# A spectral filter with two feed-forward networks: filter units over 48 slots, spectrum sums on VectorE, output gate turned on TensorE

## The chip, the cores and the metric

One Trainium2 chip, one core of it. The engines are TensorE (PE in the profile, with its weight loads as PEld), VectorE (DVE), ScalarE (ACT), GpSimd (POOL) and SyncE (SP, which here only issues DMAs). The metric is the time of one execution on the device in microseconds, the median of the runs shown.

## The reference

```python
def _attn_ref(x, filt_r, filt_i):            # x: 8 x 3072 x 256
    X = np.fft.rfft(x, axis=1)
    y = np.fft.irfft(X * (filt_r + 1j * filt_i)[None], n=x.shape[1], axis=1)
    return y.astype(np.float32)

def _moe_ref(x, w_in, w_out):                # 24576 x 256 -> 2048 -> 256
    h = x @ w_in
    g = np.where(h > 0.0, h, np.exp(np.minimum(h, 0.0)) - 1.0)
    return (g @ w_out).astype(np.float32)

def _moe2_ref(x, w_gate, w_output_gate, w1, w2):   # 8 experts, 256 -> 1024 -> 256
    logits = x @ w_gate
    e_idx = np.argmax(logits, axis=1)
    ...
    gate_w = probs[np.arange(N), e_idx]
    eom = 1.0 / (1.0 + np.exp(-(x @ w_output_gate)))
    for e in range(E):
        mask = e_idx == e
        h = np.maximum(x[mask] @ w1[e], 0.0)
        out[mask] = gate_w[mask, None] * eom[mask, e, None] * (h @ w2[e])
```

The three follow each other: a filter along the sequence for 8 batches, a feed-forward network, and a network of 8 experts in which each token goes to one.

## The kernel before

The program has three stages. The **start** filters batch 0, from which the second stage takes its first input. Its order comes from the compiler's scheduler. The **main loop** has 768 slots; its order is written out by hand. The **expert stage** works through the tokens in about 100 blocks of 256; the change leaves it alone but for where the table of the output gate comes from.

**A slot of the main loop.** 48 chunks of 512 tokens have 16 slots each. Slot t runs, in this order: the side work planned for it, `mm1(t)` (6 matmuls of 512 columns into one of two PSUM buffers `h`, then on ScalarE a Relu and an Exp into `e`, then on VectorE the step `e`, which reads `h` and so frees it), `split_g(t-1)` (a rounded copy of `e` on ScalarE and the rest, `g`, on VectorE), and `mm2(t-3)` (12 matmuls of 264 columns into four accumulators `z`). Side work marked for TensorE stands at the slot's end. Each engine works in order, so side work of slot t on VectorE stands ahead of step `e` of slot t; `mm1(t+2)` needs the `h` that step `e` of slot t frees. Once in 16 slots come the emptying of `z` into `rt`, the gate (`gate1` to `gate3`) and the scatter of rows to DRAM by GpSimd, and VectorE's two halves of the next chunk's input (`ys`, L637); every 11 slots a piece of the experts' weights is prepared (`prep_*`, with L767 on GpSimd).

**A filter unit** is one half (128 columns) of one batch, b = 1 to 7, two for each 96 slots. Its parts:

- `fft.load`: 16 DMAs of x into tile `X` (1.5 MB).
- `f1`, `f2`: 12 and 9 VectorE steps of 128 to 1536 elements, from `X` through `AA` into `AT` (L173 to L195).
- six pairs of frequencies, each through `PAIR`: `ld` (tables `cf`, filter `fl`), `hi`, `lo`, `neg`, `fwd` (12 matmuls), `mul` (VectorE, with the filter), `add` and `ylo` (GpSimd, L285, L286, L299), `yhi`, `inv` (12 matmuls with table `ci`), `evac`.
- `b1`: 20 steps of VectorE that join the pairs' results in `Z`, and two DMAs to `yd`, from which later chunks are loaded.

`plan_unit` puts `f1` in slots t0 to t0+7, `f2` in t0+8 and t0+9, pair i in t0+9+3i and on, `b1` in t0+33 to t0+42, three pieces of `f1` in two slots and two of `b1` in one; units of a batch start 43 slots apart, and 10 of 96 slots have none. `cf`, `fl`, `ci`, `X`, `AT` and `Z` have one buffer each. SyncE issues nearly all DMAs from one queue, in order.

**The output gate.** The expert stage needs `w_output_gate` with its rows and columns exchanged (`wogT`). A DMA from GpSimd's queue does that at the start, element by element (L921).

Of the kernel before, what the change touches and what calls it, by code (L numbers as in the profile page):

```python
# [9 lines left out]
F32 = mybir.dt.float32  # L10
F32R = mybir.dt.float32r
# [5 lines left out]
ALU = mybir.AluOpType  # L17
# [14 lines left out]
R8 = float(np.sqrt(0.5))  # L32
S3 = float(np.sqrt(0.75))
# [60 lines left out]
class Fft:  # L94
# [35 lines left out]
    def unit(self, b, h, own=None):  # L130
# [4 lines left out]
        nc, one, st, big = self.nc, self.one, self.st, self.big  # L135
        v, tt, stt = nc.vector, nc.vector.tensor_tensor, nc.vector.scalar_tensor_tensor
# [64 lines left out]
        P = {}  # L201
# [79 lines left out]
        def add(i):  # L281
            p = P[i]
            a, c = p["a"], p["b"]
            Y = p["Y"] = a
            nc.gpsimd.tensor_tensor(out=Y[:, :, 0], in0=a[:, :, 0], in1=c[:, :, 1], op=ALU.subtract)  # L285
            nc.gpsimd.tensor_tensor(out=Y[:, :, 1], in0=a[:, :, 1], in1=c[:, :, 0], op=ALU.add)  # L286

        def yhi(i):
            p = P[i]
            if not own:  # L290
                off, n = self.off[i]
                k = p["k"] = st.tile([W, 1792], F32R, tag="ci", name="ci")
                nc.sync.dma_start(out=k[:, 0:n].bitcast(F32), in_=self.inv_d[:, off:off + n])
# [101 lines left out]
        def eight(q, e, w):  # L395
# [142 lines left out]
def fft_moe_kernel(ctx, tc, x, filt_r, filt_i, w_in, w_out, wg, wog, w1, w2, out):  # L538
    nc = tc.nc
    v, g = nc.vector, nc.gpsimd  # L540
# [11 lines left out]
    wogT = dram.tile([NE * W, D], F32, name="wogT")  # L552
# [4 lines left out]
    ident = ct[:, 88:216]  # L557
# [10 lines left out]
    def bank():  # L568
        return pf.tile([W, 512], F32, tag="pf", name="pf")
# [36 lines left out]
    P1 = {}  # L606
# [13 lines left out]
    Y = {}  # L620
# [148 lines left out]
    def prep_st(n):  # L769
# [22 lines left out]
    def plan_unit(b, h, t0, nxt, early=False):  # L792
        u = fft.unit(b, h)
        late = {}
        for n, q in enumerate(u["f1"]):
            late.setdefault(t0 + n * 8 // len(u["f1"]), []).append(q)
        for n, q in enumerate(u["f2"]):
            late.setdefault(t0 + 8 + n // 5, []).append(q)
        if nxt:
            late.setdefault(t0 + 10, []).append(lambda: fft.load(*nxt))  # L800
        for t, fns in late.items():
            for fn in fns:
                at(t, fn)
        for t in range(9, 33):
            for i in range(6):
                for nm, d in sorted(PAIR, key=lambda q: -q[1]):
                    if 9 + 3 * i + d == t:
                        at(t0 + t, lambda nm=nm, i=i: u[nm](i), nm in ("fwd", "inv"))
# [59 lines left out]
    cf, ci = {}, {}  # L868
# [414 lines left out]
```

## Time and profile before

| | |
|---|---|
| time, median of 3 runs | 3935.37 us (3932.18 to 3935.83) |
| the profiled execution | 3930.68 us, its span 3928.8 us |
| TensorE busy | 3730.6 us, 95% of the span |
| VectorE busy | 2426.4 us, 62% |
| ScalarE busy | 2071.2 us, 53% |
| GpSimd busy | 908.9 us, 23% |
| granted clock, mean of the span | 0.987 |
| start, to the first matmul of `mm1` | 137.8 us |
| main loop | 137.8 to 2702.1 us |
| expert stage | 2702.1 to 3928.8 us |

Busy shares are averages over the three stages; a matmul counts as busy to its modelled end, so 95% doesn't say that nothing can be gained.

### The profile page before, as it was taken

The numbers are of one execution on the slowest core, as the hardware profiler recorded it, in microseconds if no ns is written. First come the engines' busy times: TensorE is split into PE (matmuls) and PEld (weight loads), VectorE is DVE, ScalarE is ACT, GpSimd is POOL, SyncE is SP. The second block draws the span as 40 slices with busy tenths as digits, with TensorE's granted clock in tenths as the row PEclk, the third lists the DMA queues.
The fourth block names the chain that finished last, engine by engine and source line by source line (L and its number), as shares of the span: only waits on it lengthen the run. The fifth ranks groups of instructions, "written<-read, shape, count | busy, mean of one in ns | idle before, by whom it ended". The sixth has DMA issues, their size and how long they took to land. (4 is left out here: it accounts for less than half of the span.)

```text
span 3928.8 us, 70310 instructions
## 1 busy us (share of the span) xinstructions
PE 3730.6 (95%) x26359; PEld 3494.2 (89%) x26359; DVE 2426.4 (62%) x4761; ACT 2071.2 (53%) x3896; POOL 908.9 (23%) x1019
## 2 busy tenths in 40 slices
PE   2799999999999999999999999997999999999998
PEld 2688998988889889899898988997999999999998
DVE  5878778777686876877868676554433433433433
ACT  2566666666666666666666666664333333333332
POOL 2532232222312223222222221111111111111111
PEclk9899999999999999999999999998999999999999
DMA  6543343333423424334243342200121221221221
GB/s 147 180 137 112 127 148 113 117 117 111 152 80 132 149 90 149 102 120 131 89 147 109 126 129 71 93 28 24 46 89 49 89 88 48 90 88 49 89 89 36
DMA packets 234945, 400.55 MB, mean 102 GB/s; under 512 B 21354, under 2 KB 153834, under 8 KB 228458
## 3 DMA queue, kind: packets, MB, share of 16 engines
q1 hardware_dynamic: 215706, 344.40, 28.4%
q0 software_dynamic: 18896, 51.62, 3.6%
q8 instruction: 210, 3.44, 0.4%
q14 instruction: 133, 1.09, 0.1%
HBM read 679.09 MB, written 114.78 MB: 202 GB/s over the span
## 5 line engine op out<-in xcount | busy, mean ns | idle before, releaser
L672 PEld LDWEIGHTS z<-wex,g 128*128 128x128 f32 x9216 | 1231.6, 189 | 85.5 <-DVE rt L690 16.8
L672 PE MATMUL z<-wex,g 128*128 128x264 f32 x9216 | 1256.7, 285 | 14.0 <-DVE rt L690 13.6
L649 PE MATMUL h<-ys,win 128*128 128x512 f32 x4608 | 1215.4, 399 | 49.0 <-DVE e L655 44.0
L649 PEld LDWEIGHTS h<-ys,win 128*128 128x128 f32 x4608 | 818.0, 189 | 201.7 <-DVE e L655 57.6
L655 DVE SCALAR_TENSOR_TENSOR e<-e,h 128x512 f32<-128x512 f32 x768 | 525.7, 684 | 643.0 <-ACT e L654 639.2
L653 ACT ACTIVATE e<-h 128x512 f32<-128x512 f32 x768 | 459.2, 598 | 687.3 <-PE h L649 644.9
L1201 PE MATMUL h<-zt,w1s 128*128 128x256 f32 x4800 | 593.4, 283 | 0.8 <-ACT zt L1169 0.7
L1218 PE MATMUL o<-w2s,hs 128*128 128x256 f32 x4800 | 585.1, 281 | 0.0
L1201 PEld LDWEIGHTS h<-zt,w1s 128*128 128x128 f32 x4800 | 583.6, 192 | 1.5 <-ACT zt L1169 1.1
L1218 PEld LDWEIGHTS o<-w2s,hs 128*128 128x128 f32 x4800 | 567.3, 188 | 0.0
L662 DVE TENSOR_TENSOR g<-e,g 128x512 fp32r<-128x512 f32 x768 | 548.9, 715 | 0.1
L654 ACT ACTIVATE e<-e 128x512 f32<-128x512 f32 x768 | 485.7, 632 | 24.4
L661 ACT CAST g<-e 128x512 fp32r<-128x512 f32 x768 | 465.7, 606 | 44.8 <-DVE e L655 44.2
L1206 DVE SCALAR_TENSOR_TENSOR hs<-h,hs 128x512 fp32r<-128x512 f32 x400 | 276.9, 692 | 313.8 <-ACT hs L1205 312.8
L1226 POOL DMA_INDIRECT out_dram<-o,rows x200 | 197.5, 988 | 994.7 <-ACT o L1225 591.1
L1205 ACT ACTIVATE hs<-h 128x512 fp32r<-128x512 f32 x400 | 239.3, 598 | 338.7 <-PE h L1201 334.8
L743 POOL DMA_INDIRECT rows_d<-rt,sl x192 | 202.8, 1056 | 555.2 <-DMA rows_d<-rt,sl 228.2
L1225 ACT ACTIVATE o<-o,ogv 128x256 f32<-128x256 f32 x200 | 84.0, 471 | 461.5 <-PE o L1218 461.5
L1181 DVE TENSOR_SCALAR ogv<-ogv 128x2 f32<-128x2 f32 x100 | 17.0, 170 | 384.9 <-ACT ogv L1180 384.9
L720 POOL TENSOR_TENSOR A<-A,ohb 128x8 bf16<-128x8 bf16 x192 | 73.9, 385 | 685.6 <-DVE rt L711 624.4
L299 POOL TENSOR_TENSOR YH<-fa,YH 128x512 fp32r<-128x512 f32 x88 | 115.3, 1310 | 209.1 <-ACT YH L295 208.3
L285 POOL TENSOR_TENSOR fa<-fa,fb 128x256 f32<-128x256 f32 x88 | 72.9, 828 | 274.1 <-DVE fa L279 148.1
(262 smaller groups left out, 3013.4 us busy)
## 6 DMA issues: line engine op xcount, KB each, us to landing
w1s<-wpk SPq DMA_DIRECT2D x200, 1024.0 KB
w2s<-wpk SPq DMA_DIRECT2D x200, 1024.0 KB
ci<-dft_inv SPq DMA_DIRECT2D x73, 768.0 KB
cf<-dft_fwd SPq DMA_DIRECT2D x87, 512.0 KB
wpk<-ps SPq DMA_DIRECT2D x64, 512.0 KB
rows<-rows_d SPq DMA_DIRECT2D x100, 258.0 KB
y<-yd SPq DMA_DIRECT2D x46, 512.0 KB
fl<-fs SPq DMA_DIRECT2D x84, 256.0 KB
```

Source lines behind the costliest of these rows:

```text
L649: nc.tensor.matmul(out=ps, lhsT=win_s(m // 4)[:, a, k, m % 4 * W:m % 4 * W + W], rhs=s[:, q, k], start=(n == 0), stop=(n == 5))
L653: nc.scalar.activation(out=e, in_=ps, func=AF.Relu, scale=-1.0)
L654: nc.scalar.activation(out=e, in_=e, func=AF.Exp, scale=-1.0)
L655: v.scalar_tensor_tensor(out=e, in0=e, scalar=-1.0, in1=ps, op0=ALU.add, op1=ALU.max)
L661: nc.scalar.copy(out=s[:, 0], in_=e)
L662: v.tensor_tensor(out=s[:, 1], in0=e, in1=s[:, 0].bitcast(F32), op=ALU.subtract)
L672: nc.tensor.matmul(out=Z[c][i], lhsT=s[:, q, i * W:i * W + W], rhs=wex_s(m // 4)[:, a, m % 4], start=(m == 0 and q == 0 and a == 0), stop= ...
L743: g.indirect_dma_start(out=rows_d, out_offset=bass.IndirectOffsetOnAxis(ap=f["sl"][:, i:i + 1], axis=0), in_=f["rt"][:, i, NE:NE + ROW], i ...
L1201: nc.tensor.matmul(out=ps[:, q * TB:q * TB + TB], lhsT=w1s[mp // 2][:, a, k, m * W:m * W + W], rhs=s[:, z, k], start=(n == 0), stop=(n == 5))
L1205: nc.scalar.activation(out=hs[:, 0, 2 * mp:2 * mp + 2], in_=p2, func=AF.Relu)
L1206: v.scalar_tensor_tensor(out=hs[:, 1, 2 * mp:2 * mp + 2], in0=p2, scalar=0.0, in1=hs[:, 0, 2 * mp:2 * mp + 2].bitcast(F32), op0=ALU.max, o ...
L1218: nc.tensor.matmul(out=pss[q], lhsT=hs[:, z, k, q * W:q * W + W], rhs=w2s[k // 4][:, a, k % 4], start=(k == 0 and n == 0), stop=(k == 7 an ...
```

## The change

It has three parts. **The plan of the units.** A unit has 48 slots and the pairs stand 4 slots apart (`GAP`). `f1` and `f2` of the next unit are done while this one's pairs run, `b1` after them is cut so that one third of it (`thirds(0, 1)`) is done among the pairs, and `level` spreads the steps by their sizes: it fills slot after slot up to a cap, counting what stands there already (`load_of`, and 1.4 us of credit where a `fwd` or `inv` makes the slot longer), and raises the cap until all fit. The loads are issued elsewhere: `X` at t0, to be used from t0+8 on; `cf` three slots ahead of its `fwd` (before two), `ci` three ahead of its `inv` (before two). **The sums and low parts of the spectrum** (`add`, `ylo`) are on VectorE, in the start too. **The output gate** is loaded as it lies, turned by two small matmuls with the identity in slot 15, copied by ScalarE and stored as rows in slot 17; the DMA at the start is gone.

```diff
         def add(i):
-            nc.gpsimd.tensor_tensor(out=Y[:, :, 0], in0=a[:, :, 0], in1=c[:, :, 1], op=ALU.subtract)
-            nc.gpsimd.tensor_tensor(out=Y[:, :, 1], in0=a[:, :, 1], in1=c[:, :, 0], op=ALU.add)
+            tt(out=Y[:, :, 0], in0=a[:, :, 0], in1=c[:, :, 1], op=ALU.subtract)
+            tt(out=Y[:, :, 1], in0=a[:, :, 1], in1=c[:, :, 0], op=ALU.add)
...
         def ylo(i):
-            nc.gpsimd.tensor_tensor(out=p["YH"][:, 1], in0=p["Y"], in1=p["YH"][:, 0].bitcast(F32), op=ALU.subtract)
+            tt(out=p["YH"][:, 1], in0=p["Y"], in1=p["YH"][:, 0].bitcast(F32), op=ALU.subtract)
...
+        def back():
+            return thirds(0, 1), [(768, b1[0]), (384, b1[1]), (384, b1[2])] + thirds(1, 3) + [
+                (1024, lambda: stt(out=w2(), in0=zvu()[:, 1], scalar=-0.5, in1=zvu()[:, 0], op0=ALU.mult, op1=ALU.add)),
+                (1024, b1[16])], [
+                (1024, lambda: stt(out=zvu()[:, 1], in0=zvu()[:, 2], scalar=-S3, in1=w2(), op0=ALU.mult, op1=ALU.add)),
+                (1024, lambda: (stt(out=zvu()[:, 2], in0=zvu()[:, 2], scalar=S3, in1=w2(), op0=ALU.mult, op1=ALU.add),
+                                b1[-1]()))]
...
+    def og_turn():
+        ps = OG["p"] = bank()
+        for k in range(2):
+            nc.tensor.matmul(out=ps[0:NE, k * W:k * W + W], lhsT=OG["t"][:, k * NE:k * NE + NE], rhs=ident, start=True, stop=True)
...
+    def level(steps, t0, t1):
+        steps = [(weight(n), fn) for n, fn in steps]
+        def fill(cap):
+            t, used, out = t0, 0.0, []
+            for k, _ in steps:
+                while load_of(t) + used + k > cap:
+                    t, used = t + 1, 0.0
+                    if t > t1:
+                        return None
+                used += k
+                out.append(t)
+            return out
...
+    UPAIR = [("ldf", 0), ("hi", 0), ("lo", 1), ("neg", 2), ("fwd", 2), ("mul", 3), ("ldk", 4), ("add", 4), ("yhi", 5),
+             ("ylo", 6), ("inv", 7), ("evac", 8)]
+    GAP = 4
...
+            free = prev + GAP * 5 + 2
+            level(f1[:6], prev + 7, free - 1)
+            level(f1[6:] + f2, free, t0 - 1)
...
+            at(t0, lambda: fft.load(*nxt))
+        t1 = t0 + GAP * 5 + 9
...
+        q0, q1, y2 = u["back"]()
+        level(q0, t0 + 13, t1 - 1)
+        level(q1, t1, t0 + 41)
+        level(y2, t0 + 42, t0 + 48)
...
-    with nc.allow_non_contiguous_dma(reason="a transpose of 8 KB, once"):
-        nc.gpsimd.dma_start(out=wogT.rearrange("(e p) d -> p e d", p=W)[0], in_=wog.rearrange("d e -> e d"))
...
+        at(12, og_ld)
+        at(15, og_turn, True)
+        at(17, og_st)
...
-                t0 = U0 + 43 * h if b == 1 else 96 * (b - 1) + 43 * h
+                t0 = (U0 + 9, U0 + 45)[h] if b == 1 else 96 * (b - 1) - 4 + 48 * h
```

VectorE in the main loop before, slots 235 to 237 (unit b = 3, second half: `f1` begins; L655 is step `e`, L662 is `g`, L637 the next chunk's input):

```order
L662 TENSOR_TENSOR g<-e,g 128x512
L173 TENSOR_TENSOR AA<-X 128x1024
L174 TENSOR_TENSOR X<-X 128x1024
L655 SCALAR_TENSOR_TENSOR e<-e,h 128x512
L662 TENSOR_TENSOR g<-e,g 128x512
L175 SCALAR_TENSOR_TENSOR X<-AA,X 128x1024
L637 TENSOR_TENSOR ys<-y,ys 128x512
L655 SCALAR_TENSOR_TENSOR e<-e,h 128x512
L662 TENSOR_TENSOR g<-e,g 128x512
L176 TENSOR_TENSOR X<-X,AA 128x1024
L177 TENSOR_TENSOR AA<-X 128x1536
L637 TENSOR_TENSOR ys<-y,ys 128x512
```

VectorE now, slots 196 to 198, where the same `f1` begins (L690 is step `e`, L697 is `g`, L292 and L293 `add`, L238 `lo`, L302 `ylo`):

```order
L697 TENSOR_TENSOR g<-e,g 128x512
L292 TENSOR_TENSOR fa<-fa,fb 128x2x128
L293 TENSOR_TENSOR fa<-fa,fb 128x2x128
L173 TENSOR_TENSOR AA<-X 128x1024
L690 SCALAR_TENSOR_TENSOR e<-e,h 128x512
L697 TENSOR_TENSOR g<-e,g 128x512
L238 TENSOR_TENSOR H<-AT,H 128x2x256
L174 TENSOR_TENSOR X<-X 128x1024
L690 SCALAR_TENSOR_TENSOR e<-e,h 128x512
L697 TENSOR_TENSOR g<-e,g 128x512
L302 TENSOR_TENSOR YH<-fa,YH 128x512
L175 SCALAR_TENSOR_TENSOR X<-AA,X 128x1024
```

The `f1` steps stand one to a slot, 39 slots earlier, among the pairs of the unit before; `add` and `ylo` are new in VectorE's queue.

GpSimd at the program's start before (L921 is the output gate's DMA, L173 and L174 belong to `f1` of batch 0's second half, L285, L286 and L299 are `add` and `ylo`):

```order
L921 DMA wogT<-in_moe_w_output_gate_dram 8x256x1
L173 ISA
L173 TENSOR_TENSOR Z<-win_120 128x1024
L174 TENSOR_TENSOR win_120<-win_120 128x1024
L285 TENSOR_TENSOR fa<-fa,fb 128x2x128
L286 TENSOR_TENSOR fa<-fa,fb 128x2x128
L299 TENSOR_TENSOR YH<-fa,YH 128x512
```

GpSimd now (L567 is the low part of a weight, L532 before; L404 a step that joins batch 0's results):

```order
L173 ISA
L173 TENSOR_TENSOR Z<-win_120 128x1024
L174 TENSOR_TENSOR win_120<-win_120 128x1024
L567 TENSOR_TENSOR win_658<-win_120,win_658 128x1024
L567 TENSOR_TENSOR wex_811<-raw,wex_811 128x4x256
L567 TENSOR_TENSOR win_846<-raw,win_846 128x1024
L404 TENSOR_TENSOR Z_118<-Z_118 128x128
```

The DMA and all of `add` and `ylo` are gone from GpSimd's queue; what is left there is in the order that it had.

## Rows read from the trace of the kernel before

**Rows 1.** Busy time by stage: start, the loop's first 96 slots, the next 576.

```profile
core 0: us, PE busy (x) PEld busy (x) DVE busy (x) ACT busy (x) POOL busy (x), PEclk, DMA share, GB/s
0.00:137.80 137.80, 54.44 (x317) 48.97 (x317) 89.14 (x139) 40.99 (x80) 56.98 (x46) 0.89 0.65 157
137.80:486.50 348.70, 325.63 (x2066) 293.24 (x2067) 275.24 (x487) 219.21 (x401) 105.75 (x114) 0.97 0.42 133
486.50:2428.40 1941.90, 1886.61 (x12194) 1715.91 (x12193) 1437.56 (x2581) 1249.73 (x2298) 503.87 (x591) 1.00 0.37 120
```

**Rows 2.** The same columns: 16 slots without a unit, 16 slots with six `fwd`/`inv`.

```profile
2611.80:2657.50 45.70, 45.70 (x292) 41.61 (x291) 24.80 (x51) 29.42 (x53) 5.33 (x9) 1.00 0.04 12
1356.50:1410.80 54.30, 54.30 (x364) 50.12 (x363) 36.12 (x65) 35.45 (x67) 17.42 (x21) 1.00 0.36 117
```

**Rows 3.** TensorE's waits in those 576 slots: us in total, times, longest.

```profile
PE h L649 <- DVE e L655: 32.1, 50, 2.6
PE z L672 <- DVE rt L690: 12.0, 12, 2.3
PE pf L256 <- DMA cf<-dft_fwd: 11.1, 7, 3.2
```

**Rows 4.** Timeline of VectorE and TensorE in one crowded slot: start, us, engine, line.

```profile
967.81 1.76 DVE L177 TENSOR_TENSOR AA<-X 128x1536 f32<-128x1536 f32 x1
970.08 0.68 DVE L655 SCALAR_TENSOR_TENSOR e<-e,h 128x512 f32<-128x512 f32 x1
970.82 1.45 PE L649 MATMUL h<-ys,win 128*128 128x512 f32 x5 [1.62 <-DVE e L655]
```

**Rows 5.** VectorE's groups in those 576 slots: busy us, mean ns | idle before.

```profile
L279 DVE TENSOR_TENSOR fa<-pf,fl 128x512 f32<-128x512 f32 x60 | 40.9, 681 | 6.1 <-POOL YH L299 6.1
L388 DVE SCALAR_TENSOR_TENSOR AA<-Z 128x1024 f32<-128x1024 f32 x12 | 14.7, 1225 | 0.4
L374 DVE TENSOR_TENSOR Z<-Z 128x384 f32<-128x384 f32 x12 | 6.6, 552 | 0.0
L191 DVE TENSOR_TENSOR AT<-X 128x256 f32<-128x256 f32 x12 | 5.1, 425 | 0.4
```

**Rows 6.** Timeline of VectorE, four steps back to back (start stage).

```profile
50.55 1.95 DVE L166 SCALAR_TENSOR_TENSOR AT<-AT 128x384 f32<-128x384 f32 x4
```

**Rows 7.** GpSimd's steps in those 576 slots: duration ns min/median/max.

```profile
L285 POOL TENSOR_TENSOR fa<-fa,fb x72: 726/742/1256, 527.7 to 2350.2; 128x256 f32<-128x256 f32 x72
L299 POOL TENSOR_TENSOR YH<-fa,YH x72: 1271/1295/1547, 533.0 to 2357.3; 128x512 fp32r<-128x512 f32 x72
```

**Rows 8.** Timeline of a VectorE step of 32 elements beside GpSimd's `add`.

```profile
1048.50 0.75 POOL L285 TENSOR_TENSOR fa<-fa,fb 128x256 f32<-128x256 f32 x1 [3.69 <-DVE fa L279]
1048.55 0.74 DVE L705 TENSOR_TENSOR ex<-rt,mx 128x32 f32<-128x32 f32 x1
```

**Rows 9.** First microseconds: SyncE's issues of batch 0's two halves, and VectorE's waits.

```profile
6.82 24.40 SPq L124 DMA_DIRECT2D X<-in_x_dram  x6
41.20 2.99 SPq L124 DMA_DIRECT2D win<-in_x_dram  x6
31.97 1.22 DVE L173 TENSOR_TENSOR AA<-X 128x1024 f32<-128x1024 f32 x1 [30.66 <-DMA X<-in_x_dram]
35.37 1.23 DVE L175 SCALAR_TENSOR_TENSOR X<-AA,X 128x1024 f32<-128x1024 f32 x1 [0.92 <-DMA X<-in_x_dram]
```

**Rows 10.** DMA issues of the first 20 us: KB each, us to landing.

```profile
wogT<-n_moe_w_output_gate_dram POOLq DMA_DIRECT2D x1, 8.0 KB, 29.2
```

**Rows 11.** Columns as Rows 1: start from its first `f1` step; first 16 slots.

```profile
32.00:142.40 110.40, 55.23 (x317) 49.25 (x317) 93.28 (x150) 41.60 (x81) 54.92 (x41) 0.84 0.63 199
137.80:215.30 77.50, 59.16 (x324) 50.44 (x325) 64.41 (x86) 42.35 (x72) 30.50 (x26) 0.86 0.43 135
```

**Rows 12.** Timeline: the issue of a table `cf`, and the `fwd` that waited for it.

```profile
1001.26 0.56 SPq L219 DMA_DIRECT2D cf<-dft_fwd  x1
1008.85 2.89 PE L256 MATMUL pf<-H,cf 128*128 128x256 f32 x12 [3.17 <-DMA cf<-dft_fwd]
```

More of the change, by code (lines that the diff above doesn't have):

```diff
@@ L413, in eight, with thirds, w2 @@
             ]
+        def thirds(q0, q1):
+            n = q1 - q0
+            z = lambda lo, hi, s=1: zvu()[:, q0:q1, lo:hi:s]
+            E = lambda: self.AA[:, 12:12 + 4 * n].rearrange("p (q u) n -> p q u n", q=n)
+            w = lambda: self.AA[:, 20:20 + 2 * n].rearrange("p (q u) n -> p q u n", q=n)
+            return [(128 * n * k, fn) for k, fn in (
+                (1, lambda: tt(out=w()[:, :, 0], in0=z(0, 1)[:, :, 0], in1=z(1, 2)[:, :, 0], op=ALU.add)),
+                (1, lambda: tt(out=w()[:, :, 1], in0=z(0, 1)[:, :, 0], in1=z(1, 2)[:, :, 0], op=ALU.subtract)),
+                (2, lambda: tt(out=E()[:, :, 0:4:2], in0=w(), in1=z(2, 4), op=ALU.add)),
+                (2, lambda: tt(out=E()[:, :, 1:4:2], in0=w(), in1=z(2, 4), op=ALU.subtract)),
+                (2, lambda: tt(out=w(), in0=z(4, 6), in1=z(6, 8), op=ALU.subtract)),
+                (2, lambda: tt(out=z(4, 6), in0=z(4, 6), in1=z(6, 8), op=ALU.add)),
+                (1, lambda: tt(out=z(6, 7)[:, :, 0], in0=w()[:, :, 0], in1=w()[:, :, 1], op=ALU.add)),
+                (1, lambda: tt(out=z(7, 8)[:, :, 0], in0=w()[:, :, 1], in1=w()[:, :, 0], op=ALU.subtract)),
+                (2, lambda: tt(out=z(0, 2), in0=E()[:, :, 0:2], in1=z(4, 6), op=ALU.add)),
+                (2, lambda: tt(out=z(4, 6), in0=E()[:, :, 0:2], in1=z(4, 6), op=ALU.subtract)),
+                (2, lambda: stt(out=z(2, 4), in0=z(6, 8), scalar=R8, in1=E()[:, :, 2:4], op0=ALU.mult, op1=ALU.add)),
+                (2, lambda: stt(out=z(6, 8), in0=z(6, 8), scalar=-R8, in1=E()[:, :, 2:4], op0=ALU.mult, op1=ALU.add)))]
+        def w2():
+            return self.AA[:, 12:20]
+        def back():
[5 more added lines that the diff above has]
+                                b1[-1]()))]
         def in_aa(lo, hi):
@@ L439, in parts @@
                     b1[-1]])
-        return dict(f1=f1, f2=f2, b1=b1, parts=parts, ld=ld, hi=hi, lo=lo, neg=neg, fwd=fwd, mul=mul, add=add, yhi=yhi, ylo=ylo, inv=inv, evac=evac)
+        return dict(f1=f1, f2=f2, b1=b1, parts=parts, back=back, ld=ld, ldf=ldf, ldk=ldk, hi=hi, lo=lo, neg=neg, fwd=fwd, mul=mul, add=add, yhi=yhi, ylo=ylo, inv=inv, evac=evac)
 def filter_steps(tc, F, filt_r, filt_i, fs, fr2):
@@ L778, in prep_st, with og_ld, og_st @@
         nc.sync.dma_start(out=dst[:, :, o:o + 512], in_=t)
+    OG = {}
+    def og_ld():
+        t = OG["t"] = P1["s"].tile([W, 512], F32, tag="pw", name="og", bufs=1)
+        nc.sync.dma_start(out=t[:, 0:2 * NE].rearrange("p (k e) -> p k e", k=2), in_=wog.rearrange("(k p) e -> p k e", p=W))
+    def og_turn():
+        ps = OG["p"] = bank()
+        for k in range(2):
+            nc.tensor.matmul(out=ps[0:NE, k * W:k * W + W], lhsT=OG["t"][:, k * NE:k * NE + NE], rhs=ident, start=True, stop=True)
+    def og_st():
+        o = OG["t"][0:NE, 2 * NE:2 * NE + D]
+        nc.scalar.copy(out=o, in_=OG["p"][0:NE, 0:D])
+        nc.sync.dma_start(out=wogT.rearrange("(e p) d -> p e d", p=W)[0], in_=o)
     plan = {}
@@ L790, in fft_moe_kernel @@
             ("inv", 7), ("evac", 8)]
-    def plan_unit(b, h, t0, nxt, early=False):
-        u = fft.unit(b, h)
[L794 to L798, printed above, removed]
-        if nxt:
[L800 to L808, printed above, removed]
+    F1_N = [1024] * 4 + [1536] * 2 + [768] * 2 + [384] * 2 + [768] * 2
@@ new lines, in fft_moe_kernel, with weight, load_of @@
+    F2_N = [384] * 4 + [256] * 2 + [128] * 2 + [256]
+    LOAD = {}
+    def weight(n):
+        return n / 960 + 0.155
+    def load_of(t):
+        if t not in LOAD:
+            LOAD[t] = {2: 0.85, 3: 1.65, 6: 1.4, 12: 0.7, 13: 0.7}.get(t % 16, 0.0)
+        return LOAD[t]
+    def level(steps, t0, t1):
[10 more added lines that the diff above has]
+            return out
+        cap = 0.5
+        while fill(cap) is None:
+            cap += 0.05
+        for t, (k, fn) in zip(fill(cap), steps):
+            at(t, fn)
+            LOAD[t] += k
@@ new lines, in fft_moe_kernel, with plan_unit @@
+    UPAIR = [("ldf", 0), ("hi", 0), ("lo", 1), ("neg", 2), ("fwd", 2), ("mul", 3), ("ldk", 4), ("add", 4), ("yhi", 5),
+             ("ylo", 6), ("inv", 7), ("evac", 8)]
+    GAP = 4
+    def plan_unit(b, h, t0, prev, nxt, early=False):
+        u = fft.unit(b, h)
+        for n, i in enumerate(ORDER):
+            for nm, d in UPAIR:
+                t = t0 + GAP * n + d
+                if nm in ("fwd", "inv"):
+                    LOAD[t] = load_of(t) - 1.4
+                elif nm in ("lo", "mul", "add", "ylo"):
+                    LOAD[t] = load_of(t) + dict(lo=0.7, mul=1.4, add=0.85, ylo=0.7)[nm]
+        f1 = list(zip(F1_N, u["f1"]))
+        f2 = list(zip(F2_N, u["f2"]))
+        if prev is None:
+            level(f1 + f2, U0, t0 - 1)
+        else:
+            free = prev + GAP * 5 + 2
+            level(f1[:6], prev + 7, free - 1)
+            level(f1[6:] + f2, free, t0 - 1)
+        for t in range(t0, t0 + 33):
+            for nm, d in sorted(UPAIR, key=lambda q: -q[1]):
+                for n, i in enumerate(ORDER):
+                    if GAP * n + d == t - t0:
+                        at(t, lambda nm=nm, i=i: u[nm](i), nm in ("fwd", "inv"))
+                    if nm == "fwd" and n < 5 and GAP * n + d + 1 == t - t0:
+                        at(t, lambda i=ORDER[n + 1]: u["ld"](i))
+        at(t0 - 1, lambda: u["ld"](0))
+        if nxt:
+            at(t0, lambda: fft.load(*nxt))
+        t1 = t0 + GAP * 5 + 9
@@ L809, in plan_unit @@
         if early:
-            p, t1 = u["parts"](v), t0 + 32
-            for n, fn in enumerate(p["q0"]):
-                at(t0 + 24 + n // 2, fn)
+            p = u["parts"](v)
+            level([(213, fn) for fn in p["q0"]], t0 + 13, t1 - 1)
             at(t1, lambda: load_half(b * 6, 0))
             for n, fn in enumerate(p["q1"]):
-                at(t1 + n // 6, fn)
+                at(t1 + n // 5, fn)
             at(t1 + 2, lambda: p["y0"](Y[b * 6][:, h]))
@@ L1058, in fft_moe_kernel @@
         plan_rest()
+        prev = None
         for b in range(1, NB):
             for h in range(2):
-                t0 = U0 + 43 * h if b == 1 else 96 * (b - 1) + 43 * h
-                plan_unit(b, h, t0, ((b, 1) if h == 0 else (b + 1, 0) if b + 1 < NB else None), b == 1 and h == 1)
+                t0 = (U0 + 9, U0 + 45)[h] if b == 1 else 96 * (b - 1) - 4 + 48 * h
+                plan_unit(b, h, t0, prev, ((b, 1) if h == 0 else (b + 1, 0) if b + 1 < NB else None), b == 1 and h == 1)
+                prev = t0
         for c in range(NC):
```

20 lines of the change are left out of this document (9 added, 11 removed).

## The prediction

> **What bounds the kernel now.** I read the busy times by stage first, then the main loop slot by slot, then TensorE's list of waits, then the start.
>
> TensorE sets the length of the main loop, and nearly nothing else does. Sixteen slots without a unit take 45.7 us with TensorE busy in all of it, so a slot is worth 2.86 us; sixteen with six `fwd` or `inv` take 54.3 us, also without a gap, so one of these adds (54.3 - 45.7) / 6 = 1.43 us [rows 2]. 96 slots with two units hold 24 of them: 6 x 45.7 + 24 x 1.43 = 308.6 us if nothing waits. The 576 slots from 486.5 us on take 1941.9 us [rows 1], 323.7 for each 96: **15 us in each, 90 in all, are stalls.** The first 96 slots take 348.7 us, 40 more than the floor, and 32 of these fall in the first 16 slots (77.5 against 45.7), where the preparing of the weights crowds VectorE [rows 1, 2, 11].
>
> What stalls is seen in the waits: step `e` of VectorE 32.1 us in 50 times, the emptying of `z`, also VectorE, 12.0, a table `cf` 11.1 [rows 3]. That is 55 of the 90; the rest I put to slower matmuls behind such a wait (12 that took 2.89 us instead of 1.43, [rows 12]) and to gaps that a modelled end hides. The timeline shows the mechanism: a step of 1536 elements, 1.76 us, and another stand ahead of step `e` in VectorE's queue, `e` ends 0.7 us after 970.08, and the next `mm1`, which needs its buffer, starts 1.62 us late [rows 4]. Yet VectorE is busy 1437.6 of 1941.9 us, 74% [rows 1]: not too much work, but work in heaps.
>
> In the start the first thing that VectorE does on x begins at 31.97 us. Six of the 16 DMAs of x kept SyncE's queue for 24.4 us, while the same six of batch 0's other half took 2.99 [rows 9]. What ran beside the first: the output gate's DMA, 8 KB, 29.2 us to land [rows 10].
>
> **The change part by part.** *The gate's DMA goes.* The six issues lose 24.40 - 2.99 = 21.4 us, and all that follows in SyncE's queue moves forward with them. If the last piece lands as soon after its issue as in the other half, L175 moves from 35.37 to about 11: 24 us. I take **-22**. What replaces it (two matmuls, one copy, two small DMAs in slots 12 to 17) lies where TensorE waits for VectorE anyway; without that cover it is under 1 us.
>
> *`add` and `ylo` on VectorE.* Durations: 681 ns for 512 elements, 425 for 256 [rows 5]; four steps of 552 ns back to back take 1.95 us, so a step in a queue costs its duration less 0.08 [rows 5, 6]. A pair adds 2 x 0.34 + 0.60 = 1.28 us to VectorE. In the start 12 pairs add 15.4 us to 93.3 busy of 110.4 [rows 11]. The 17 idle us could take it all, and GpSimd's slower steps leave the chain; or VectorE, which has other waits that no order fills, grows by most of it. Between -4 and +12, I take **+4**, nearer the idle time.
>
> In the loop 96 slots get 12 x 1.28 = 15.4 us; cutting `b1` into thirds adds 24 instructions at about 0.08: 1.9. VectorE goes from 239.6 us for 96 slots to 257, of at least 309: 83%. So it fits, if it lies well.
>
> A rule to weigh here: the trace has a step of 32 elements at 0.74 us where GpSimd's `add` runs [rows 8], while 256 elements alone take 0.43 [rows 5]; but `add` itself has a median of 742 ns, 16 above its least, and `ylo` 1295, 24 above [rows 7], so the two engines seldom meet. The Trainium skill, SBUF — State Buffer, section Who interferes with whom, says that a VectorE instruction with two SBUF inputs and a GpSimd one that reads SBUF lock each other out, the later one for the whole of the earlier. By that alone each pair would free VectorE for up to 2.8 us and the move would cost it nothing, so that the sum would be nearer to its bound of no stalls (-90 below instead of -78); by the rows the meetings are few and I count no gain.
>
> *The plan.* Before, `f1` of a unit put 2 steps of 1024 into slot t0, one of each 1024 and 1536 into t0+2. With 1.2 us for `e` and `g`, and the gate's small steps at 0.1 each (an estimate by the same line of prices), that makes 3.5, 2.3, 4.0 and (with emptying and gate) 4.3 us in four slots of 2.86: 14.1 against 11.4. Now I add up each slot's steps by the same prices against 2.86, or 4.29 where a `fwd` or `inv` ends it. The fullest: t0+7 4.2 of 4.29, t0+8 3.0 of 2.86, t0+9 2.9 of 2.86, t0+14 4.2 of 4.29, t0+19 4.3 of 4.29; 48 slots hold 118 us of 154. Two slots are over, by 0.1 each, and what follows has room. So step `e` is hardly late anywhere. What stays are meetings with GpSimd's L767 and small lags: I take 2 us for 96 slots, 12 in all, so **-78**; the bounds are no stall left (-90) and, as a third of the slots have less than 0.5 us of air, 6 to 7 us for 96 slots (-50). What is late next is TensorE itself.
>
> *The loads.* `cf` took 7.6 us from issue to its `fwd`, beside a load of `X` [rows 12]; it had two slots and now has three and the slot of its `fwd`, about 11 us, and comes ten us behind `X`, so its 11 us of waits should go (part of the 90). `X` is issued at t0 and wanted at t0+8, 8 x 2.86 + 3 x 1.43 = 27 us later; its issues took 8 us in the start's other half. Hidden. Behind it in SyncE's queue only `cf`, due 10 us later.
>
> *The first 96 slots.* The first 16 keep their steps and their heap; slots 15 to 18 get a new one as `f1` and `f2` must end by slot 19. After that the plan helps. Of the 8 us outside the heap I take **-3** (-8 to +5). The rest of the loop and the experts' stage have no edited step: 0.
>
> Sum on the profiled execution: 3930.7 - 22 + 4 - 78 - 3 = 3832. The median of the runs stands 4.7 us above that execution, so **3836**.
>
> **The rivals.**
> 1. *VectorE becomes the bound.* In the fullest slots nothing is left for a meeting with GpSimd (a small step took 0.74 us in one, [rows 8]), and mul, add and ylo now wait in one queue for matmuls and ScalarE. If half of the 90 us stays, the start takes the whole 12 and the first 96 slots grow by 2: 3930.7 - 22 + 12 - 45 + 2 + 4.7 = 3882. If VectorE's 17 us for 96 slots all come on top of TensorE, 6 x 17 eats the whole gain: about 3935, no change. For it: 83%. Against it: the sums above. The Trainium skill, Perfetto Trace Analysis, section Optimizing Scalar/DVE Operations, has it that with VectorE saturated moving work to GpSimd may make sense, though the two share a read port; by it this part goes the wrong way, which would be this rival; at 74% the trace does not yet call VectorE saturated.
> 2. *The start isn't shorter*: x crawls for another cause, or VectorE's added work takes it all: 3836 + 22 = 3858. Against it: the issues run at full pace from the moment that the 8 KB have landed.
> 3. *Slower: `X` comes late.* It has 27 us where it had over 90. VectorE would stop at `f1`'s first step with `e` behind it, in each of 12 to 13 units. To eat 99 us a unit must lose 7.6, so the point is a load of 35 us. The start's first load took that long, but beside the 8 KB DMA; 8 us of issue speak against it. With 40 us: 3836 + 13 x 13 = 4005.
>
> **How the numbers follow.** Forecast with its bounds (3808 to 3866): 0.75. Rival 1: 0.11, of which 0.08 leaves a gain, 0.02 none and 0.01 a loss. Rival 2: 0.06. Rival 3: 0.04. Still faster than the bounds: 0.04. The range 3806 to 3882 holds the forecast, rival 2 and the lighter part of rival 1. A measurement of this kernel tells about 0.2%, 8 us. Faster 0.93 (forecast, rival 2, most of rival 1, the faster rest), same 0.02, slower 0.05.
>
> **What would show it.** First `f1` step near 9 to 11 us instead of 32; first `mm1` near 120 instead of 137.8. 96 slots of the loop in 309 to 313 us, VectorE busy about 255 of them; `mm1` waiting for step `e` under 10 us in the 576 slots, `fwd` for `cf` near 0. Wrong would be: slots over 3 us at t0+7 to t0+9 or t0+14 to t0+19 with `e` as the releaser (rival 1), VectorE waiting for `X` (rival 3), a start as long as before (rival 2).

## The result, and the profile after

The changed kernel takes **3821.89 us** (median of 4 runs, 3820.19 to 3823.33) against 3934.87 for the kernel before on the same chip: ratio 0.9714, 95% interval 0.9697 to 0.9731. The profiled execution took 3822.26 us, its span 3820.5.

Busy time by stage after: start, the loop's first 96 slots, the next 576, the rest of the loop, the experts; then the first 16 slots and the last 16, which have no unit. The columns are those of [rows 1].

```profile
0.00:114.80 114.80, 54.23 (x316) 49.40 (x316) 95.07 (x174) 41.08 (x80) 16.95 (x9) 0.84 0.66 197
114.80:468.60 353.80, 329.29 (x2082) 296.69 (x2083) 305.12 (x558) 221.56 (x404) 71.61 (x78) 0.97 0.44 136
468.60:2324.70 1856.10, 1856.10 (x12183) 1701.99 (x12182) 1513.13 (x2919) 1244.61 (x2295) 294.96 (x375) 1.00 0.39 124
2324.70:2598.40 273.70, 273.70 (x1731) 248.06 (x1731) 149.95 (x304) 177.17 (x314) 40.06 (x60) 1.00 0.15 51
2598.40:3820.50 1222.10, 1190.79 (x10057) 1188.37 (x10056) 474.10 (x1252) 384.08 (x807) 201.87 (x208) 0.99 0.23 70
...
114.80:191.90 77.10, 60.00 (x328) 51.02 (x328) 63.99 (x87) 42.37 (x71) 30.04 (x26) 0.86 0.40 123
...
2508.00:2553.80 45.80, 45.80 (x293) 41.68 (x292) 24.79 (x51) 29.50 (x54) 5.54 (x9) 1.00 0.04 13
```

Against [rows 1]: the start is 23.0 us shorter, the first 96 slots 5.1 longer, the 576 slots 85.8 shorter; the rest of the loop is the same, and the experts' 1222.1 stand against 1226.7 (3928.8 - 2702.1), 4.6 less. The sum, 108.3, is the difference of the spans. In the third line TensorE is busy in all of its 1856.1 us, at a granted clock of 1.00, while VectorE has gone from 1437.6 to 1513.1 us: 82% of the stage instead of 74, and TensorE never waits for it there. A quiet slot [rows 2] and the first 16 slots [rows 11] have not changed.

TensorE's waits of the whole span after (engine, buffer, line, releaser: us in total, times, longest). The same list for the 576 slots alone has no entry left, where [rows 3] had three.

```profile
PE zf L263 <- ACT H L234: 27.0, 3, 21.8
PE zf L263 <- DVE H L238: 13.2, 4, 9.1
PE h L684 <- DVE e L690: 13.0, 11, 4.0
PE pf L1275 <- DMA rows<-rows_d: 8.7, 1, 8.7
...
PE z L707 <- DVE rt L725: 3.0, 2, 2.8
```

The two waits for `zf` belong to the start; those for step `e` and for the emptying of `z` lie in the first 96 slots.

The slot after that answers to the crowded one of [rows 4]: the timeline of VectorE and TensorE around the 1536-element step.

```profile
815.54 1.75 DVE L177 TENSOR_TENSOR AA<-X 128x1536 f32<-128x1536 f32 x1
...
817.04 1.56 PE L684 MATMUL h<-ys,win 128*128 128x512 f32 x6
817.21 0.68 DVE L690 SCALAR_TENSOR_TENSOR e<-e,h 128x512 f32<-128x512 f32 x1
```

One large step stands ahead of `e`; `mm1` of the slot starts on time, and nothing in these lines has a wait beside it.

VectorE's groups after in the 576 slots (as [rows 5]): the product with the filter, and the three steps that came from GpSimd (L293 is half of `add`, L302 `ylo`).

```profile
L302 DVE TENSOR_TENSOR YH<-fa,YH 128x512 fp32r<-128x512 f32 x72 | 50.6, 703 | 0.0
...
L286 DVE TENSOR_TENSOR fa<-pf,fl 128x512 f32<-128x512 f32 x59 | 40.1, 679 | 0.0
L293 DVE TENSOR_TENSOR fa<-fa,fb 128x256 f32<-128x256 f32 x72 | 31.1, 432 | 0.0
L292 DVE TENSOR_TENSOR fa<-fa,fb 128x256 f32<-128x256 f32 x72 | 30.1, 418 | 0.0
```

They cost 703, 432 and 418 ns, less than the 1295 and 742 that GpSimd took for the same shapes [rows 7].

The start after: SyncE's issues of x, both halves, and VectorE's first steps.

```profile
5.16 2.99 SPq L124 DMA_DIRECT2D X<-in_x_dram  x6
...
8.22 1.23 DVE L173 TENSOR_TENSOR AA<-X 128x1024 f32<-128x1024 f32 x1 [6.91 <-DMA X<-in_x_dram]
...
11.24 1.23 DVE L175 SCALAR_TENSOR_TENSOR X<-AA,X 128x1024 f32<-128x1024 f32 x1 [0.54 <-DMA X<-in_x_dram]
...
17.73 2.99 SPq L124 DMA_DIRECT2D win<-in_x_dram  x6
```

The six issues that took 24.40 us in [rows 9] take 2.99, as long as those of the other half, and L175 starts at 11.24 instead of 35.37.

A table `cf` and the `fwd` that uses it, after (as [rows 12]): 12.6 us lie between issue and use, and `fwd` runs in 1.60 us.

```profile
648.18 0.33 SPq L220 DMA_DIRECT2D cf<-dft_fwd  x1
660.82 1.60 PE L263 MATMUL pf<-H,cf 128*128 128x256 f32 x12
```

### The profile page after: what moved, and what is told of

It reads as the page before. It is cut to its first block, busy times and chain, and to the rows that moved or that the text cites. A ratio compares the mean times of both kernels' runs of the same rounds, so it can differ in the third digit from the quotient of the medians.

```text
span 3820.5 us, 70286 instructions
## 1 busy us (share of the span) xinstructions
PE 3704.1 (97%) x26363; PEld 3484.5 (91%) x26363; DVE 2537.4 (66%) x5205; ACT 2068.5 (54%) x3897; POOL 625.4 (16%) x730
## 5 line engine op out<-in xcount | busy, mean ns | idle before, releaser
L690 DVE SCALAR_TENSOR_TENSOR e<-e,h 128x512 f32<-128x512 f32 x768 | 525.8, 685 | 480.4 <-ACT e L689 465.9
L697 DVE TENSOR_TENSOR g<-e,g 128x512 fp32r<-128x512 f32 x768 | 544.7, 709 | 0.1
L778 POOL DMA_INDIRECT rows_d<-rt,sl x192 | 204.0, 1062 | 772.9 <-DVE sl L774 340.4
L802 POOL TENSOR_TENSOR ps<-pw,ps 128x512 fp32r<-128x512 f32 x64 | 88.1, 1377 | 369.8 <-ACT ps L797 352.3
L316 PE MATMUL pf<-ci,YH 128*128 128x256 f32 x528 | 130.3, 282 | 1.5 <-ACT YH L298 1.5
```

The source lines that it names most:

```text
L690: v.scalar_tensor_tensor(out=e, in0=e, scalar=-1.0, in1=ps, op0=ALU.add, op1=ALU.max)
L697: v.tensor_tensor(out=s[:, 1], in0=e, in1=s[:, 0].bitcast(F32), op=ALU.subtract)
L778: g.indirect_dma_start(out=rows_d, out_offset=bass.IndirectOffsetOnAxis(ap=f["sl"][:, i:i + 1], axis=0), in_=f["rt"][:, i, NE:NE + ROW], i ...
```

## The experiments

All kernels in one table: median, ratio to the kernel before with its interval, and from each profiled execution the four stages that differ (the rest of the loop is 273.7 us in all). Each ratio is to the kernel before as it ran beside that kernel, where its median was 3932 to 3939 us; so ratios are to be compared rather than medians.

```
kernel       median   ratio (95%)              start  first 96  576 slots  experts
before       3934.87  1                        137.8   348.7    1941.9    1226.7
after        3821.89  0.9714 (0.9697, 0.9731)  114.8   353.8    1856.1    1222.1
e_gate       3904.17  0.9925 (0.9909, 0.9942)  113.5   350.0    1942.8    1222.3
e_sums       3933.19  1.0002 (0.9992, 1.0012)  141.7   350.9    1940.9    1228.0
e_plan       3852.57  0.9796 (0.9779, 0.9812)  138.7   353.6    1856.1    1227.8
e_nosums     3820.49  0.9714 (0.9698, 0.9731)  112.8   352.6    1856.0    1222.4
e_packed     3843.47  0.9760 (0.9744, 0.9776)  114.3   353.3    1878.6    1221.4
e_cf2        3824.88  0.9710 (0.9694, 0.9726)  116.3   354.1    1856.1    1223.1
e_gatelate   3831.46  0.9727 (0.9711, 0.9744)  116.6   356.9    1856.0    1227.4
e_xlate      3826.47  0.9714 (0.9698, 0.9730)  115.4   359.2    1856.0    1221.7
e_late       3837.08  0.9744 (0.9729, 0.9759)  114.0   364.8    1859.8    1223.1
e_gap3       3824.94  0.9712 (0.9697, 0.9727)  114.6   355.4    1857.0    1222.4
e_first      3821.17  0.9704 (0.9691, 0.9717)  112.4   350.7    1856.0    1222.9
e_old        3952.42  1.0053 (1.0037, 1.0070)  113.9   376.5    1964.1    1222.3
```

Kernels with the sums and the gate both changed start between 112.4 and 116.6 us, so a difference of 2 us in that column says nothing.

**The gate alone, the sums alone, the plan alone.** Each takes its part of the diff ahead of the prediction; nothing else is edited.

> The kernel before with the output gate's part of the change alone: loaded as it lies in slot 12, turned by two matmuls, stored as rows. Theory G (the element-by-element DMA of 8 KB held SyncE's first loads of x up): first f1 step near 9 to 11 us instead of 32, first mm1 21 to 24 us earlier, and all later stages as before: 3935 - 22 = 3913 us, 3908 to 3917. Rival (x is late for another cause, or the start's gain is lost again in the crowded first 16 slots, which begin with the same heaps): 3930 to 3938 us.

> The kernel before with add and ylo on VectorE alone; plan and gate are those of before. Theory P (VectorE's heaps make the stalls, the plan ends them): 17 us more of VectorE work for every 96 slots, in slots that were crowded already, so nothing is gained and up to half of it is lost: 3935 to 3970 us, mm1 waiting for step e 32 us or more in the 576 slots. Rival V (GpSimd's slow steps in the chain of a pair, and its meetings with VectorE, make the stalls): a third to two thirds of the 90 us goes, 3875 to 3905 us, and the waits of mm1 fall below 20 us.

> The kernel before with the plan of the units alone (pairs four slots apart, levelled steps, loads issued earlier); add and ylo stay on GpSimd, the gate's DMA stays at the start. Theory P: the 576 slots lose 75 to 86 us, the start nothing: 3845 to 3862 us. Rival V (the sums' move to VectorE is what ended the stalls): less than half of that goes, 3890 us or more, with VectorE waiting for GpSimd's add and ylo and inv coming late.

The gate alone gives 24.3 us in the start, as theory G said, and 4.4 in the experts' stage, which it did not say. The plan alone gives the whole 85.8 us of the 576 slots, with `add` and `ylo` still on GpSimd: rival V falls. The sums alone change nothing. Theory P's loss is not there either: the stage took 1940.9 us with VectorE at 1509.2 busy, and the waits of `mm1` hardly moved (list as in [rows 3]).

```profile
PE h L649 <- DVE e L655: 35.3, 51, 2.6
PE z L672 <- DVE rt L690: 11.6, 11, 2.3
PE pf L256 <- DMA cf<-dft_fwd: 8.8, 4, 3.1
```

So 72 us more of VectorE work found room even in the old order: the sums stand among the pairs, and there the old slots were not over.

**The change without the sums.**

```diff
-            tt(out=Y[:, :, 0], in0=a[:, :, 0], in1=c[:, :, 1], op=ALU.subtract)
+            nc.gpsimd.tensor_tensor(out=Y[:, :, 0], in0=a[:, :, 0], in1=c[:, :, 1], op=ALU.subtract)
```

(and the same for the other half of `add` and for `ylo`).

> The changed kernel with add and ylo back on GpSimd: plan and gate without the sums. Theory P: the sums' place is worth little once the steps are levelled: VectorE has 17 us less for every 96 slots but nothing waits for it, 3815 to 3832 us, within 0.3% of the changed kernel. Rival V: 3850 us or more. A third way: the first 96 slots, which are VectorE's, gain from its 17 us less, 3812 to 3818 us.

The time is that of the changed kernel: theory P. What was not expected is VectorE's own time. The window of its 576 slots, with the columns of [rows 1]:

```profile
465.40:2321.40 1856.00, 1856.00 (x12182) 1701.97 (x12181) 1535.38 (x2702) 1244.95 (x2294) 540.20 (x591) 1.00 0.39 124
```

VectorE's group of the large `lo` in them (busy us, mean ns):

```profile
L238 DVE TENSOR_TENSOR H<-AT,H 128x512 fp32r<-128x512 f32 x47 | 73.0, 1552 | 0.0
```

And the timeline of one `lo` beside GpSimd's `ylo`:

```profile
624.12 1.36 POOL L302 TENSOR_TENSOR YH<-fa,YH 128x512 fp32r<-128x512 f32 x1 [1.26 <-ACT YH L298]
624.25 1.52 DVE L238 TENSOR_TENSOR H<-AT,H 128x256 fp32r<-128x256 f32 x1
```

VectorE is busy 1535.4 us in 2702 instructions; with the sums it is 1513.1 in 2919. 217 instructions more, 22 us less. In the new plan `lo` of one pair stands next to `ylo` of the pair before, and a `lo` that starts 0.13 us into GpSimd's step ends 0.29 us after it: 1.52 us. The large form of `lo` takes 1552 ns on average here and 707 in the changed kernel.

**Steps packed instead of levelled.**

```diff
-        for t, (k, fn) in zip(fill(cap), steps):
+        for n, (k, fn) in enumerate(steps):
+            t = min(t1, t0 + n // 2)
             at(t, fn)
-            LOAD[t] += k
+            LOAD[t] = load_of(t) + k
```

> The changed kernel with level made to pack: the same ranges of slots, pairs and loads, but the steps of a range stand two to a slot from its beginning on. Theory H (spreading by size is what ends the stalls): two steps of 1024 and more beside e, g and a part of a pair overfill a slot again, four to eight slots of 96 by 0.5 to 2.5 us each: 30 to 80 us of the 86 come back, 3850 to 3900 us, with mm1 waiting for step e. Rival L (the earlier loads and the slots between the pairs end them; where the steps lie hardly counts): 3815 to 3832 us.

22.5 us came back in the 576 slots, less than theory H's 30 to 80, more than rival L's none. Nearly all of it, 20.6 us, lies in two slots of each unit. VectorE and TensorE there:

```profile
800.82 1.22 DVE L176 TENSOR_TENSOR X<-X,AA 128x1024 f32<-128x1024 f32 x1
801.96 0.68 DVE L690 SCALAR_TENSOR_TENSOR e<-e,h 128x512 f32<-128x512 f32 x1
802.69 1.66 PE L684 MATMUL h<-ys,win 128*128 128x512 f32 x6 [0.58 <-DVE e L690]
803.16 0.68 DVE L238 TENSOR_TENSOR H<-AT,H 128x512 fp32r<-128x512 f32 x1
803.76 1.75 DVE L177 TENSOR_TENSOR AA<-X 128x1536 f32<-128x1536 f32 x1
805.54 1.76 DVE L178 TENSOR_TENSOR X<-X 128x1536 f32<-128x1536 f32 x1
807.22 0.68 DVE L690 SCALAR_TENSOR_TENSOR e<-e,h 128x512 f32<-128x512 f32 x1
807.95 1.66 PE L684 MATMUL h<-ys,win 128*128 128x512 f32 x6 [0.73 <-DVE e L690]
```

Two steps of 1024 after a slot that was full already make `e` late by 0.6 us for `mm1`; two of 1536 behind a `lo`, 4.1 us ahead of the next `e`, cost 0.7 more. The other packed slots are as long as in the changed kernel to within 0.1 us, but for single ones (up to 0.4).

**Loads, distance, and where the steps stand.** Four kernels undo one thing each and stay levelled. The table `cf` two slots ahead:

```diff
-                    if nm == "fwd" and n < 5 and GAP * n + d + 1 == t - t0:
+                    if nm == "fwd" and n < 5 and GAP * n + d + 2 == t - t0:
```

> The changed kernel with the table cf issued two slots ahead of its fwd, as before the change, instead of three. By the prediction's step on the loads: cf took 7.6 us beside a load of X and two slots and its fwd's own give 5.7 to 7.1 us, so a fwd beside an X load waits up to 3 us: 11 us of waits come back, 3828 to 3840 us, fwd waiting for cf about 11 us. Rival (pairs four slots apart and X issued elsewhere take cf away from X's loads): no wait, 3818 to 3826 us.

`X` four slots later:

```diff
-            at(t0, lambda: fft.load(*nxt))
+            at(t0 + 4, lambda: fft.load(*nxt))
```

> The changed kernel with the next unit's load of X issued at t0+4 instead of t0, which leaves f1's first step at t0+7 or t0+8 only 11 to 14 us. If X needs what its six issues took in the start and a little (8 to 12 us): 3820 to 3830 us, hardly a wait. If it needs the 27 us that the prediction allowed for it: VectorE stops 12 to 15 us in 12 units, 3950 to 4000 us. From the trace of the changed kernel (issue to landing beside cf and rows) I expect in between: 3 to 8 us a unit, of which step e's slack takes a part: 3840 to 3900 us.

Pairs three slots apart:

```diff
-    GAP = 4
+    GAP = 3
```

> The changed kernel with pairs three slots apart, as before the change, and everything else levelled around them (cf is then two slots ahead again). Theory among: the distance of the pairs is worth little, since the freed slots behind them take the steps: 3815 to 3835 us. Rival distance (mul, lo, add and ylo of a pair fill three slots to 2.7 us of 2.86 to 4.29, and ScalarE's hi, neg, yhi and evac come late): slots at the pairs over 3 us, 25 to 60 us back, 3845 to 3880 us.

The steps kept out of the pairs:

```diff
-            level(f1[:6], prev + 7, free - 1)
-            level(f1[6:] + f2, free, t0 - 1)
+            level(f1 + f2, free, t0 - 1)
...
-        level(q0, t0 + 13, t1 - 1)
-        level(q1, t1, t0 + 41)
+        level(q0 + q1, t1, t0 + 41)
```

> The changed kernel, still levelled, but with VectorE's side work of a unit kept out of the pairs: the first third of b1 after them (t0+29 to t0+41) instead of among them, and all of the next unit's f1 and f2 from t0+22 on instead of f1's first six from t0+7. Theory among (most of the 86 us came from giving VectorE's side work the slots of the pairs, which packing left as it was): about 45 us of steps and 31 of e and g now stand in 26 slots of 2.86 us and a few fwd or inv, 82 in 78, so 4 to 7 us a unit are lost, 12 units: 3865 to 3910 us, mm1 waiting for e. Rival loads (the earlier X and cf and the levelling ended the stalls, the pairs' slots do not count): 3815 to 3832 us.

None of them brings the stalls back: the 576 slots take 1856.0 to 1857.0 us in the first three and 1859.8 in `e_late`. My expectation for `e_xlate` was far off: `X` does with the 11 to 14 us that it has left, and VectorE never waits for it in those slots; the 4.6 us of the median are in the first 96. Rival "distance" falls with `e_gap3`, theory "among" with `e_late`: 26 slots behind the pairs are enough, and 11 of its 15 us are in the first 96 slots (364.8), where there is less room. Each relief could be taken away by itself at hardly any cost; so either the others make up for it, or it had no part.

**The old places of the steps, with everything else new.**

```diff
-            level(f1[:6], prev + 7, free - 1)
-            level(f1[6:] + f2, free, t0 - 1)
+            for n, (_, fn) in enumerate(f1):
+                at(t0 - 10 + n * 8 // 12, fn)
+            for n, (_, fn) in enumerate(f2):
+                at(t0 - 2 + n // 5, fn)
...
-        level(q0, t0 + 13, t1 - 1)
-        level(q1, t1, t0 + 41)
-        level(y2, t0 + 42, t0 + 48)
+        b1 = q0 + q1 + y2
+        for n, (_, fn) in enumerate(b1):
+            at(t1 + n * 10 // len(b1), fn)
```

> The changed kernel with the loads, the pairs' distance, the sums and the gate as they are, but VectorE's side work of a unit where the kernel before had it: f1 in the eight and f2 in the two slots ahead of the pairs, all of b1 in the ten slots behind them, none of it levelled. The earlier variants took one part away at a time and each cost 0 to 23 us, so that two explanations of the remaining 60 us stand. Theory windows (any one relief is enough, and all of the 86 us was VectorE's work in windows that are too narrow: f1 and f2 take 17 us, e and g 12, gate or ys 2 to 3 more, 32 in ten slots of 2.86 us; b1 with its own e, g and gate some 30): 4 to 7 us a unit come back, 3870 to 3905 us, mm1 waiting for e. Rival others (the loads, the pairs' distance and the even spacing of the units did the larger part together): no more than the packed variant lost, 3835 to 3850 us.

It is slower than the kernel before, by 0.5%: 108 us came back in the 576 slots and 23 in the first 96. But not as either theory had it. Most slots of the windows cost little here: they are 0.1 to 0.3 us over on average, single ones up to 1.2. Nearly all the loss, 103 us, is one place in each unit, where the end of `b1` and the beginning of the next `f1` meet ahead of the emptying of `z`. TensorE's waits for the emptying in the 576 slots (as in [rows 3]), and the timeline of one such place:

```profile
PE z L707 <- DVE rt L725: 70.5, 12, 6.5
```

```profile
771.19 1.22 DVE L392 TENSOR_TENSOR Z<-Z 128x1024 f32<-128x1024 f32 x1
...
776.10 1.23 DVE L174 TENSOR_TENSOR X<-X 128x1024 f32<-128x1024 f32 x1
777.24 0.68 DVE L690 SCALAR_TENSOR_TENSOR e<-e,h 128x512 f32<-128x512 f32 x1
...
778.44 0.77 DVE L725 COPY rt<-z 128x264 f32<-128x264 f32 x2
...
778.92 2.13 PE L707 MATMUL z<-wex,g 128*128 128x264 f32 x8 [6.04 <-DVE rt L725]
...
780.85 2.55 PE L684 MATMUL h<-ys,win 128*128 128x512 f32 x6
```

Five steps of 1024 (L392 to L174, 6.1 us) stand ahead of `e` and `rt`. TensorE waits 6.0 us, and the next `mm1` takes 2.55 instead of 1.56; in this slot, 770.73 to 780.85, the granted clock was 0.77 on average, a mixture of the two levels of 1.2 and 2.4 GHz: in its last part, from 779.00 on, it was 0.50, the lower one, after TensorE had stood idle from 772.9 to 778.9. Over the 576 slots TensorE is busy 1887.5 us here for the work that takes 1856.1 in the changed kernel: 31 of the 108 us are slower matmuls, 77 are waits.

This place is not one that the kernel before had. There `b1` began 24 slots behind the first pair and the units stood 43 or 53 slots apart, so that `b1` ended in a slot ahead of the next `f1`. With pairs 4 apart it begins 29 slots behind, the units stand 48 apart, and the last three steps of `b1` share a slot with the first two of the next `f1`. So this kernel shows what a heap of 6.1 us costs. It does not show what the old places cost in the old spacing, and no kernel here has that spacing together with the rest of the change.

**The gate's DMA, but late.** `og_ld`, `og_turn` and `og_st` go, and this stands in slot 12:

```diff
+            nc.gpsimd.dma_start(out=wogT.rearrange("(e p) d -> p e d", p=W)[0], in_=wog.rearrange("d e -> e d"))
```

> The changed kernel with the output gate's element-by-element DMA of 8 KB again, but issued in slot 12 of the loop instead of at the start; the turn on TensorE is gone. Theory place (what cost 23 us was that the first loads of x waited beside it): the DMA takes its 29 us where nothing waits for it, 3815 to 3830 us. Rival DMA (such a DMA holds up any load beside it by some 20 us): tables, filter and X of slots 12 to 22 come late and the first 96 slots grow by 10 to 20 us, 3832 to 3842 us.

Theory "place" holds for the start: with no load of x beside it the DMA costs nothing there (116.6 us is within the scatter), and the first 96 slots take 3.1 us more. The total, 3831.46, lies at the edge of both ranges: of the 10.2 us by which the profiled span is longer than the changed kernel's, 5.3 lie 2400 us later, in the experts' stage (last section).

**Two slots more for the first unit.**

```diff
-            level([(213, fn) for fn in p["q2"]] + [(1024, fn) for fn in p["y2"][:2]] + [(0, p["y2"][2])], t1 + 5, t1 + 16)
+            level([(213, fn) for fn in p["q2"]] + [(1024, fn) for fn in p["y2"][:2]] + [(0, p["y2"][2])], t1 + 5, t1 + 12)
...
-                t0 = (U0 + 9, U0 + 45)[h] if b == 1 else 96 * (b - 1) - 4 + 48 * h
+                t0 = (U0 + 11, U0 + 47)[h] if b == 1 else 96 * (b - 1) - 4 + 48 * h
```

> The changed kernel with both units of batch 1 two slots later (pairs from slots 22 and 58) and the early unit's last steps done by t1+12. In the changed kernel slots 17 to 20 lose about 6.5 us to the 21 steps of f1 and f2 that must end by slot 19; two slots more give VectorE 3 to 4 us of room: 2 to 5 us less, if the crowded slots 87 to 93 (2.5 us over) do not grow by as much: 3816 to 3823 us, at the edge of what a measurement tells. Rival: what crowds slots 11 to 19 is the preparing of the weights alone, no change within 2 us.

The first 96 slots take 350.7 us instead of 353.8, as expected, but the median of 3821.17 can't be told from the changed kernel's. No kernel here is measurably faster than the change; the change without its sums ties with it.

## Why the prediction was right, and where not

The forecast was 3836 us, the measurement 3821.9. Of the 14 us, 4.7 are the distance of the median from the profiled execution, which I carried over; after, the two agree within 0.4. The rest is in the terms, and it is small partly by luck: the start came out 5.0 us shorter than the sum had it, the 576 slots 7.8 and the experts 4.6, but the first 96 slots 8.1 longer, which offsets the plan's miss. The terms:

- **The gate's DMA, -22**: right. Issues, landing and first step moved as worked out, and `e_gate` gives -24.3 in the start.
- **VectorE's work in the start, +4**: the sums raise VectorE's busy time there from 83.2 to 95.1 us, and the start by 3.9 (`e_sums`) or 2.0 (`e_nosums` against after). Both are near the scatter of that column; the bound of +12 is excluded.
- **The plan, -78** (-85.8 measured): the mechanism was right, its residue mis-sized. I left 2 us for 96 slots to meetings and lags; there is nothing that TensorE's list shows. That the loss was heaps can be read in the kernel before slot by slot: from each slot's first `mm1` to the next, less 2.86 us, or 4.30 with a `fwd` or `inv`, and summed over the 576 slots, 87 us are left over. 43 of them lie where `f1` and `f2` run (17 and 26 for the two halves), 27 at `b1`, 12 in the one slot of 96 where `fwd` waited for `cf`, and 5 at the other pairs. The same sum after is 3 us. `e_packed` and `e_old` bring losses back by heaps alone, with heaps of 4.1 and 6.1 us ahead of `e`. That the plan as a whole ends the stalls is shown by `e_plan`; which of its parts did it is not. One part was never tried alone: the units' new spacing, which every kernel with the plan has. It may matter, for 37 of the 87 us lie in slots 3 to 5 of a chunk, behind the emptying of `z` and beside the gate, and 20 in slots 12 to 15, with and behind the `ys` steps; the new spacing puts the units' steps elsewhere against this work, and `level` counts it.
- **The sum per slot as the test**: I took two slots to be over by 0.1 us. A slot may be well over for a moment: most of the packed slots and `e_late`'s 26 cost nearly nothing, so the levelled plan had more air than this term said.
- **No gain from fewer meetings with GpSimd**: right for the time, wrong for VectorE's work. In the old order the sums add 71.6 us to it in the 576 slots (`e_sums`), 20 less than the 6 x 15.4 that I counted. In the new order, where the plan moves `lo` beside `ylo`, VectorE loses 22 us more to the meetings without the sums than the sums themselves cost it. The Trainium skill, SBUF — State Buffer, section Who interferes with whom, says that a VectorE instruction with both inputs in SBUF and a GpSimd one that reads SBUF exclude each other, and that the one issued later stands still meanwhile; the 1.52 us of `lo`, which has both inputs there, agree with it. So I had looked on the wrong side: GpSimd's own durations [rows 7] tell nothing of the meetings in which VectorE came second, as in [rows 8], where `add` took 0.75 us, near its median, while VectorE's small step took 0.74. It moved no time, because TensorE waits for VectorE in those slots neither with the sums (`after`) nor without them (`e_nosums`).
- **The loads**: `cf` waits no more, as said, but not for the reason given. Two slots ahead do as well (`e_cf2`). In the 576 slots of `e_old` heaps are back and no `fwd` waits for `cf`, so that the likelier reason is that `X` no longer stands beside it; that was not tried alone.
- **The first 96 slots, -3**: wrong in sign, +5.1. The plan alone does it (353.6 in `e_plan`, 350.0 in `e_gate`). 1.4 us is a `fwd` of the next unit that now falls into slot 94. I had named the new heap in slots 15 to 18 but offset it by a gain behind it; `e_first` gives back 3.1 with two slots more for it.
- **The experts' stage, 0**: wrong by 4.6, from the gate's DMA (below).

Rival 1 (VectorE becomes the bound) had 82% of busy time for it and did not come; rival 2 and rival 3 fell with `e_gate` and `e_xlate`.

## What to carry to other kernels

In this kernel, with two buffers between TensorE and VectorE, neither VectorE's busy share nor the fullness of a whole stretch set the time, but the heaps that stood ahead of the steps that free a buffer: look for the slots that are over, and what stands in them. Where several steps can be spread, any one relief may do, so undo them together as well as singly before you say which of them mattered. A DMA that moves single elements should not run beside loads that something waits for: here it held up six issues by 21 us. And work that nothing waits for, as `add` and `ylo` here, could be moved to VectorE and back at no cost in time.

## What the runs showed that was not expected

**One DMA of GpSimd at the start costs 5 us at the end.** The experts' stage takes 1226.7 to 1228.0 us in the four kernels that issue the gate's element-by-element DMA from GpSimd (before, `e_sums`, `e_plan`, `e_gatelate`), wherever it stands, and 1221.4 to 1223.1 in the ten that don't. About 2.5 us of it come at the stage's beginning, where GpSimd scatters the last rows, and 2.9 behind the last matmul (15.9 us from its end to the end of the span in `e_gatelate`, 13.0 after). The fourth scatter in `e_gatelate`, then in the changed kernel:

```profile
2625.89 0.97 POOL L778 DMA_INDIRECT rows_d<-rt,sl  x1 [4.89 <-issue]
```

```profile
2618.27 0.97 POOL L778 DMA_INDIRECT rows_d<-rt,sl  x1 [2.23 <-DMA rows_d<-rt,sl]
```

The wait is 2.7 us longer, and no releaser is shown for it. Why an earlier DMA on that queue does this was not found out.
